# A kernel laid out by a planner: the planner's DMA model refitted, the early order searched again, two more blocks of x transposed by DMA

## The chip, the cores and the metric

The kernel runs on one core of a Trainium2 chip. The metric is the device time of one execution in microseconds (us), the median of several. Executions come with a state; only fast ones are compared, and where a profiled execution was of the slow state the text says so. TensorE is written PE, VectorE DVE, ScalarE ACT, GpSimd POOL, SyncE SP.

## The reference

Sliding-window attention with eight global keys, then a two-layer network with softplus on its output. Cut to what matters:

```python
# q, k, v: [4 batches, 8 heads, 768, 64];  w_in: [512, 2048];  w_out: [2048, 512]
scores = scale * q @ k^T + bias          # kept: 8 global keys, and the 96 keys up to the query
a      = softmax(scores)                 # bias: -slope[head] * distance
attn   = a @ v
x      = attn.transpose(0, 2, 1, 3).reshape(3072, 512)
h      = x @ w_in
out    = (relu(h) + log1p(exp(-abs(h)))) @ w_out        # softplus(h) @ w_out
```

## The kernel before

The 3072 tokens are 24 blocks of 128, or 12 windows of two blocks. For each window q, k and v are loaded (512 KB each), cast to bf16, transposed; each block gets scores, exp, the product with v (PV), a normalization and a transpose, which makes a piece of x. A window of x is then multiplied with w_in, goes through softplus and is multiplied with w_out. w_in and w_out come in four quarters of 512 KB each, cast on the way by GpSimd's DMA queue; everything else is loaded by SP's queue. Windows are counted from 0 in names.

No engine's order is written down by hand (the code below is shortened, cuts are marked by "..."). Some 900 operations, each with an engine, an estimated duration, what it needs and a rank, are put into an event simulation while the program is built. It issues at each engine the ready operation of lowest rank, and **the order that comes out is the order of the program**. In the traces DVE never overtakes: what stands first and waits holds up all behind it (in run e5 below DVE stands 4.32 us in front of one cast, and everything behind it comes later).

```python
SEEN = {"pe": 0.22, "dve": 0.1, "act": 0.1, "pool": 0.1, ...}     # us until another engine sees the end

def move(self, now):                      # model of the DMA engines: queues take turns, packet by packet
    heads = [q[0] for q in self.moving.values() if q]
    cycle = sum(h[2] for h in heads) / 1e3
    step = min(min(h[1] for h in heads), (now - self.moved) / cycle)
    ...
    op.end = self.moved + 0.7             # landed
    self.at(op.end + op.slack, lambda op=op: self.done(op))

def plan(self, busy):
    ...                                   # for each engine that is free at `now`:
    op = self.pick(e)                     # the ready operation of lowest rank
    if op is None and e == "pe" and now < self.filler_until: op = Op("filler", ...)   # multiplies zeros
    self.order.append(op)
    first = now + 1.3 if e == "sp" else op.end + 1.2      # first packet of a DMA
...
POOL_ORDER = "q1 in0 in1 out0 q2 out1 in2 in3 out2 out3".split()  # weights; "q1": wait for load q1
SP_ORDER = "in1 w2 in2 w3".split()        # "in1": wait for that quarter; "w2": load window 2
...
dur, dma = 0.55 * f + 0.05, (64 * f, 28)                          # a load of q, k or v
landed[s] = pl.add(f"w_{side}{s}", "pool", 0.78, ..., dma=(32, 98))   # a quarter: 32 packets, 98 ns each
...
f"castq{w}", {"dve": 0.69}, after=loaded[w, "q"]                  # cast of q of a window
f"oc{g}_{ns}", "dve", 0.69, after=[mm2s[g, last], ...], frees=[(mm2s[g, last - 3], "O")]
                                          # copy of an output block out of the one bank o_ps
for op in plan:
    op.fn(op)                             # emits the instructions in the planned order
```

`castq` waits for a load, and the copy `oc` frees the only bank that w_out products of the next output block can write.

The softmax here doesn't subtract the row's maximum and nothing guards it: scores larger than these inputs give would overflow.

## Time and profile before

| | before |
|---|---|
| median of 4 executions, and range | 219.44 us, 218.36 to 219.75 |
| span of the profiled execution | 217.1 us |
| first product with w_in | 18.46 us |
| PE's time lost in 0–24 / 24–60 / 60–84 / 84–98 / 98–120 / 120–132 / 132–end us | 11.08 / 1.59 / 0.31 / 0.38 / 0.30 / 0.11 / 0.90 |
| planned and real issue of the load of q7, us | 80.46, 81.51 |
| planned and real landing of q7, us | 84.59, 86.81 |

The loss is PE's spacing from one product to the next less the price of its kind, as the prediction prices them, with time for products of zeros counted as lost. I use 400 w_out records as the full count (11 windows of 32 and a last of 48), of which 31 lack a record in this trace (the prediction counted 384 and put 15 back, which comes to the same time, for of the last 48 some are narrower). Three of the 16 bias products lack a record too, all before 24 us; they are put back at 0.216 us each. The prediction counted 13, so its loss before 24 us is 0.65 us too large. "Planned" is the planner's own time for the operation; "real" is the trace's.

The prediction shows the page's rows and the start. Here is what it did not show, DVE's timeline around 87 us (start, length, line, operation):

```profile
86.83 0.69 DVE L564 COPY osb<-o_ps 128x512 f32<-128x512 f32 x1
87.55 1.23 DVE L424 TENSOR_TENSOR z<-s_ps,biasA 128x1024 f32<-128x1024 f32 x1
88.69 0.68 DVE L293 CAST qb<-q 128x1024 bf16<-128x1024 f32 x1
```

The copy of the output block comes first, then a bias addition, then the cast of q7. q7 landed at 86.81, 2.2 us later than planned, and nobody noticed. The table by stretch (us, PE, PEld, DVE, ACT, POOL, clock, DMA share, GB/s) has PE full there:

```profile
84.00:98.00 14.00, 13.84 (x150) 9.81 (x152) 11.13 (x21) 11.55 (x16) 5.53 (x9) 1.00 0.86 192
```

### The profile page before, as it was taken

How to read it: one execution, taken by the hardware profiler on the slowest of the kernel's cores; microseconds unless marked ns; L12 is line 12 of the kernel's file. 1: busy time of each engine (PE TensorE's matmuls, PEld its weight loads, DVE VectorE, ACT ScalarE, POOL GpSimd, SP SyncE). 2: the span in 40 equal slices, each digit the busy share in tenths (PEclk: the TensorE clock that was granted, in tenths of full speed). 3: DMA queues.
4: the chain of work that ended last, by engine and by line, in shares of the span. 5: the costliest groups of instructions: out<-in, count | busy, mean ns of one | idle time of the engine just before them, and what ended most of it. 6: DMA issues, size and time to landing. Idle time of an engine off the chain costs nothing.

```text
span 217.1 us, 5047 instructions
## 1 busy us (share of the span) xinstructions
PE 207.8 (96%) x2035; PEld 145.8 (67%) x2069; DVE 116.9 (54%) x251; ACT 156.0 (72%) x208; POOL 60.3 (28%) x117
## 2 busy tenths in 40 slices
PE   7599999999999999999999999999999999999994
PEld 6377875766677666667767767666766766776542
DVE  6575644728696685885544854654764763110120
ACT  4476885995969957888959669668768758857700
POOL 3570190014727170640404350332360000000000
PEclk9999999999999999999999999999999999999999
DMA  5999999999999986959577874987791211201102
GB/s 155 298 217 200 276 149 196 212 305 266 194 267 264 211 193 203 250 89 255 89 157 213 167 165 151 210 188 206 154 211 51 75 24 51 72 0 48 53 38 106
DMA packets 71511, 35.98 MB, mean 166 GB/s; under 512 B 27328, under 2 KB 68544, under 8 KB 71488
## 3 DMA queue, kind: packets, MB, share of 16 engines
q1 hardware_dynamic: 67120, 31.27, 62.1%
q0 software_dynamic: 4224, 4.19, 12.2%
q8 instruction: 16, 0.26, 0.5%
q10 hardware_dynamic: 144, 0.20, 0.2%
q14 instruction: 7, 0.06, 0.1%
HBM read 27.26 MB, written 6.29 MB: 155 GB/s over the span
## 4 chain that ended last, share of the span: by engine, by line
PE 82%; DMA 12%; SPq 2%; issue 1%; POOL 1%; ACT 0%; DVE 0%
PE h_ps L492 36%; PE o_ps L520 31%; DMA q<-in_q_dram 6%; PE s_ps L393 5%; PE x_ps L448 4%; DMA w_in_bf<-in_moe_w_in_dram 3%; PE s_ps L545 3%; DMA w_out_bf<-in_moe_w_out_dram 3%; PE s_ps L520 3%; SPq L286 1%; PE h_ps L470 0%; PE o_ps L545 0%; PE h_ps L319 0%; PE x_ps L445 0%; POOL w_in_bf L574 0%
## 5 line engine op out<-in xcount | busy, mean ns | idle before, releaser
L492 PE MATMUL h_ps<-XT,w_in_bf 128*128 128x256 bf16 x768 | 96.4, 273 | 0.3 <-ACT e L503 0.3
L492 PEld LDWEIGHTS <-w_in_bf 128*128 128x128 bf16 x768 | 73.2, 98 | 20.8 <-DMA w_in_bf<-in_moe_w_in_dram 0.5
L503 ACT ACTIVATE e<-h_ps 128x512 f32<-128x512 f32 x96 | 59.0, 629 | 29.5 <-PE h_ps L492 29.2
L520 PE MATMUL o_ps<-w_out_bf,g 128*128 128x512 bf16 x291 | 77.7, 379 | 1.4
L511 ACT ACTIVATE g<-e 128x1024 bf16<-128x1024 f32 x48 | 50.6, 1055 | 0.8
L520 PEld LDWEIGHTS <-g 128*128 128x128 bf16 x352 | 31.9, 98 | 23.8 <-issue 0.4
L430 ACT ACTIVATE pb<-z 128x1024 bf16<-128x1024 f32 (+1 forms) x40 | 39.1, 984 | 8.2 <-DVE z L424 7.9
L424 DVE TENSOR_TENSOR z<-s_ps,biasA 128x1024 f32<-128x1024 f32 x34 | 40.8, 1220 | 6.8 <-PE s_ps L393 6.2
L459 DVE RECIPROCAL rcp<-x_ps 128x4 f32<-128x4 f32 x44 | 7.9, 180 | 42.8 <-PE x_ps L448 38.8
L302 POOL CAST vb<-v 64x512 bf16<-64x512 f32 (+1 forms) x44 | 26.4, 600 | 14.0 <-DMA v<-in_v_dram 12.0
L302 POOL CAST kb<-k 64x512 bf16<-64x512 f32 x32 | 20.0, 627 | 34.9 <-DMA k<-in_k_dram 33.7
L564 DVE COPY osb<-o_ps 128x512 f32<-128x512 f32 x20 | 13.7, 686 | 25.7 <-PE o_ps L520 25.0
L460 DVE TENSOR_TENSOR xs<-x_ps,rcp 128x256 bf16<-128x256 f32 x44 | 18.7, 424 | 1.5
L448 PEld LDWEIGHTS <-pb 128*128 128x128 bf16 x320 | 14.5, 97 | 4.0
L393 PEld LDWEIGHTS <-kT 64*128 64x128 bf16 x352 | 10.0, 94 | 8.4 <-issue 7.2
L393 PE MATMUL s_ps<-qT,kT 64*128 64x128 bf16 x352 | 15.1, 218 | 0.0
L448 PE MATMUL x_ps<-vb,pb 128*128 128x65 bf16 x288 | 14.6, 193 | 0.0
L362 POOL COPY kT<-kT 128x32 bf16<-128x32 bf16 x16 | 3.3, 209 | 39.8 <-issue 20.2
L371 DVE COPY vb<-vb 4x512 bf16<-4x512 bf16 x32 | 10.3, 322 | 0.5
L434 ACT ACTIVATE pb<-s_ps 128x1024 bf16<-128x1024 f32 (+1 forms) x8 | 7.2, 916 | 4.6 <-PE s_ps L393 4.6
L293 DVE CAST qb<-q 128x1024 bf16<-128x1024 f32 x10 | 6.9, 690 | 5.3 <-DMA q<-in_q_dram 5.2
L646 PE MATMUL o_ps<-zeros 128*128 128x128 bf16 x85 | 8.0, 251 | 1.0 <-DVE zeros L599 1.0
(62 smaller groups left out, 97.6 us busy)
## 6 DMA issues: line engine op xcount, KB each, us to landing
out_dram<-osb SPq DMA_DIRECT2D x23, 256.0 KB, 2.6
q<-in_q_dram SPq DMA_DIRECT2D x11, 512.0 KB, 5.3
k<-in_k_dram SPq DMA_DIRECT2D x11, 512.0 KB, 5.7
v<-in_v_dram SPq DMA_DIRECT2D x11, 512.0 KB, 5.0
w_in_bf<-in_moe_w_in_dram POOLq DMA_DIRECT2D x4, 512.0 KB, 7.9
w_out_bf<-in_moe_w_out_dram POOLq DMA_DIRECT2D x4, 512.0 KB, 11.1
q<-in_q_dram SPq DMA_DIRECT2D x2, 256.0 KB, 4.3
k<-in_k_dram SPq DMA_DIRECT2D x2, 256.0 KB, 4.6
```

Source lines behind the costliest of these rows:

```text
L302: copy_on[eng](dst[64 * r : 64 * r + 64, hs, :], src)
L371: nc.vector.tensor_copy(vb_of(n - 1)[sl, :, 0:D], vb_of(first)[sl, :, 0:D])
L393: nc.tensor.matmul(s_t[:, 4 * sub + (lh // 2 if i == 0 else 2 * (lh // 2) + b), :], k_of(n - b, rows, m), q_of(n, rows, m), start=begin, s ...
L424: nc.vector.tensor_tensor(packed(n, z), rows_of(n, s_t), bias, ALU.add)
L430: nc.scalar.activation(pb[:, 0:nr, :], z[:, 0:nr, :], AF.Exp, scale=1.0 / root_d)
L448: nc.tensor.matmul(xv[:, lh, :], pb[:, 2 * j + b, :], vb_of(n - b)[:, h, :], start=b == 0, stop=b == 1,)
L460: nc.vector.tensor_tensor(xs[:, 4 * half : 4 * half + 4, :], xv[:, :, 0:D], rcp[:][:, :, None].to_broadcast([P, 4, D]), ALU.mult,)
L492: nc.tensor.matmul(hv[:, j, :], w_in_bf[:, m, fb * P : fb * P + P], XT[:, m, W * g : W * g + W], start=(m == 0), stop=(m == NM - 1),)
L503: nc.scalar.activation(e[:, p % 2, :].rearrange("p (a t r) -> p a r t", a=4, r=2), state["h", g, p][:].rearrange("p (a r t) -> p a r t", a ...
L511: nc.scalar.activation(gt[:, 4 * c : 4 * c + 4, :].rearrange("p a t -> p (a t)"), state["e", g, c][:].rearrange("p a t -> p (a t)"), AF.Ln ...
L520: nc.tensor.matmul(dst, state["g", g][:, fb, ns * P : ns * P + P], w_out_bf[:, fb, :], start=(fb == 0), stop=(fb == NFB - 1),)
L564: copy_on[eng](osb[:], src)
```

## The change

The intent: fit the planner's DMA model to traced transfers of the start, so that PE's order there meets the data where they really land; with the better model search a new early order of loads and weights; take eight more transposes from PE; halve four late loads. The arithmetic is the same. The diff, cut to its core:

```diff
+RANKS = {"Tq3.0": 9.51, "mm2_1_1.0": 10.15, ..., "mm1_0_0.0": -13.91, ...}    # 29 shifts of rank
+HALVED = "v10 q11 k11 v11".split()
+EARLY, MERGED, T_DMA, X_DMA = 4, 6, 4, 6
+SP_ORDER = "q0a k0a v0a k0b q0b q1 k1 v0b v1 in1 q2 k2 in2 k3 v2 q3 v3"
+POOL_ORDER = "q1 in0 in1 out0 in2 q2 in3 out1 out2 out3"
-    POOL_ORDER = "q1 in0 in1 out0 q2 out1 in2 in3 out2 out3".split()
-    SP_ORDER = "in1 w2 in2 w3".split()
+BASE = (-1.41, -18.64, 15.76, ...)            # other ranks of the first 14 blocks
+    LAP = {"dve": 0.08, "act": 0.1, "pool": -0.05, ...}    # an engine's next may start this early
+    FIRST = {"sp": 1.3, "pool": 1.9}                       # first packet after issue (pool: 1.2 before)
+    SLOW, SLOWER, SKEW = (3.6, 5.4), 1.8, 0.5              # slower packets early; landings + 0.5 to 51 us
-            f"w_{side}{s}", "pool", 0.78, lambda op: fn(s), rank, behind=[gate], dma=(32, 98)
+            f"w_{side}{s}", "pool", 0.78, lambda op: fn(s), rank, behind=[gate], dma=(32, 82)
-        if n < 8:                             # x transposed on PE
+        if n < X_DMA:                         # else by a transposing DMA
-                    after=[lns[0, p // 2], landed_out[...], mm2s.get((0, p - 1))],
+                    after=[lns[0, p // 2], landed_out[...]], behind=[mm2s.get((0, p - 1))],
...                                            # a few durations by 0.01 to 0.05 us
```

## The prediction

> **What bounds the kernel now.** I read the page first, then the table by stage, the timeline of TensorE over the first 60 us, the landings of the early transfers, and the list of waits. The page's busy and slice rows:
>
> ```profile
> PE 207.8 (96%) x2035; PEld 145.8 (67%) x2069; DVE 116.9 (54%) x251; ACT 156.0 (72%) x208; POOL 60.3 (28%) x117
> PE   7599999999999999999999999999999999999994
> DMA  5999999999999986959577874987791211201102
> ```
>
> TensorE (PE) is full from the third slice to the last (one slice is 5.4 us), and no other engine comes near. The DMA engines are full over the same early stretch, until slice 15, about 76 us. But a busy PE need not be doing useful work. The table by stage, first for all instructions (us, PE, PEld, DVE, ACT, POOL, clock, DMA share, GB/s), then for line 646 alone, which multiplies zeros to keep PE's clock up:
>
> ```profile
> 0.00:18.46 18.46, 14.43 (x199) 11.43 (x202) 12.17 (x49) 10.14 (x14) 8.83 (x26) 1.00 0.97 221
> 18.46:24.00 5.54, 5.49 (x85) 4.54 (x83) 3.13 (x12) 5.06 (x6) 0.42 (x2) 1.00 1.10 218
> 60.00:180.00 120.00, 118.90 (x1181) 83.16 (x1201) 75.87 (x144) 91.89 (x123) 36.98 (x67) 1.00 0.76 171
> ```
> ```profile
> 0.00:18.46 18.46, 7.76 (x83) 6.53 (x83) 1.00 0.97 221
> ```
>
> Of the 85 filler products 83 are before 18.46 us, where the first product with w_in starts. To get PE's useful work I priced each kind by its spacing in dense stretches of the timeline: 109 ns for a w_in product (256 columns), 216 ns for a w_out product (512), about 35 for a score, 30 for a PV product, 55 for a transpose, 216 or 109 for a bias product. Times the counts, with the 15 missing w_out records put back: 768 x 0.109 = 83.9; 384 x 0.216 = 82.9; 352 x 0.035 = 12.3; 352 x 0.030 = 10.6; 96 transposes 5.3; 13 bias products 2.3; 197 us together. PE's last product ends at 213.9, so 16.9 us are lost, and the closing copy and store take 3.2. Where the 16.9 lie, by summing the same prices window by window: 4.9 in 0 to 6 us, 4.2 in 6 to 12, 2.7 in 12 to 18, 0.9 in 18 to 24, about 2 in 24 to 60 (0.3 of it looks like a missing record), about 2.2 spread over the 150 us that follow. The start is therefore where there is something to win, and the rest is nearly bare work.
>
> Where 12 to 24 us goes, from PE's timeline (start, length, line, operation):
>
> ```profile
> 15.96 0.52 PE L470 MATMUL h_ps<-ident,xs 128*128 128x128 bf16 x4
> 16.32 1.22 PE L646 MATMUL o_ps<-zeros 128*128 128x128 bf16 x19
> 17.38 0.59 PE L378 MATMUL s_ps<-biasA,ident 128*128 128x512 bf16 x2
> 17.81 0.39 PE L646 MATMUL o_ps<-zeros 128*128 128x128 bf16 x4
> 18.13 0.40 PE L393 MATMUL s_ps<-qT,kT 64*128 64x128 bf16 x8
> 18.46 1.05 PE L492 MATMUL h_ps<-XT,w_in_bf 128*128 128x256 bf16 x8
> ```
>
> PE multiplies zeros 23 times (23 x 56 ns = 1.3 us) while w_in's first quarter, by its semaphore, landed at 17.13 and x of block 1 is out by 17.1 (copy at 16.69, 0.42 long). The first w_in product was simply put late in a fixed order. The second loss, in 30 to 48 us:
>
> ```profile
> 36.04 1.64 PEld L492 LDWEIGHTS <-w_in_bf 128*128 128x128 bf16 x16 [0.52 <-DMA w_in_bf<-in_moe_w_in_dram]
> 42.43 0.75 PEld L492 LDWEIGHTS <-w_in_bf 128*128 128x128 bf16 x7 [0.37 <-issue]
> ```
>
> w_in's third quarter (landed 36.00) is waited for half a microsecond, and once the exp that frees an h bank is late.
>
> **What the Trainium skill says.** Perfetto Trace Analysis, Identifying the Most-Contended Engine: matmul busy share is a poor measure of how near the roofline one is, and LDWEIGHTS busy share is a good one. The trace agrees in kind: 207.8 busy includes 8.0 us of fillers and overlapping tails, LDWEIGHTS is at 67%, so I count by spacing. TensorE: Matmul & The Clock Gate, Back-to-back issue gap: N/2.4 + 2.5 ns between isolated warm products, 109.2 for 256 columns and 215.8 for 512; the trace has just these spacings (8 in 0.87, 4 in 0.86), and not the lower ones that the same section gives for pipelined streams. DMA: Bandwidth & Descriptors, Issuing engines are not separate DMA queues: whatever engine issues, the transfers share the 16 engines and interleave. The trace agrees: q2, k2, v2 took 5.5 to 7.7 us to land from SP's queue beside the weights of GpSimd's queue, against 1.8 us of spacing between full loads while these had the engines alone (11.39, 13.18). So reordering transfers moves a landing only at the cost of another, except where the engines idle.
>
> **The change, part by part.** No arithmetic changes. The kernel's instruction streams are laid out by a planner while the program is built; the chip then follows that order and never reorders.
>
> (1) Order of early loads: k0's second half, q0's second half, q1, k1, then v0's second half, v1 (before: all of window 0 first). Landings before: 7.83, 8.71, v0's second half 9.60, q1 11.39, k1 13.18, v1 14.83. A half takes 0.88. So q1 should land at 10.5, k1 12.3, v0's second half about 13.2 or a little later, v1 15 to 16. The weights' gate is q1, so they are issued 0.9 earlier (10.7 instead of 11.57). But the bytes that must pass before w_in quarters 0 and 1 are complete are the same, and the engines have no gap there: quarter 0 stays at 16.5 to 17, quarter 1 at 19.3 to 19.7. Price: half 1 of blocks 0 and 1 waits for v: 13.2 + casts 0.7 + PV 0.3 + two normalizations 1.2 + transpose 0.4 + copy 0.6 = 16.4, still just before the weights.
>
> (2) Refitted planner: a weight packet 82 instead of 98, other latencies, new ranks for 29 operations, -13.91 among them for the first w_in product. It should now stand where its data land, 16.8 to 17.3 instead of 18.46. Gain: the 1.3 us of fillers seen above, less some for an order that misses: **1.2 us**.
>
> (3) w_in quarter 2 moves ahead of q2 into the first batch of weights, k3 follows it on SP before v2, q3, v3. Before, between 19.73 (quarter 1) and 29.40 (v2) 9.7 us passed for one w_out quarter (about 2.8) and three loads (5.4): some 1.4 us of DMA idle, which the longer queue fills. Quarter 2 lands at 26 to 28 instead of 36.0, window 3 some 5 us earlier; v2 comes later (34 to 37 instead of 29.4), but x of blocks 4 and 5 is first used by the products at 50.7, so that costs nothing. Gain: the 0.5 wait at 36.0 and a part of the other 1.2 us lost in 24 to 60: **0.6 us**.
>
> (4) x of blocks 7 and 8 (counted from one) by DMA: 8 PE transposes go, 8 x 55 ns = **0.44 us**, all of it on PE, which sets the end there. Two PSUM copies (0.42 on DVE, 0.58 on ACT) go too, beside other work. Two transposing DMAs come, 3.2 us to landing each in the median; x of these blocks is made around 60 to 64 us and used at 68.5, so hidden.
>
> (5) Four more halved loads (v10, q11, k11, v11): the same bytes in more DMAs, after 100 us, where the DMA share is 0.75 and less. PE waits for no load there: **0**.
>
> (6) `behind` instead of `after` between w_out products, scheduling overlaps, other estimates: planning only; order after 60 us changes a little. Only 2.2 us is lost there, so 0, plus or minus 0.4.
>
> Sum: 1.2 + 0.6 + 0.44 = 2.2, less 0.2 for small misses: 2.0 us off 219.27 gives **217.3 us**.
>
> **Rivals.** (A) The new wait takes the place of the old: v0's second half moves 3.6 us back and the margin computed in (1) is under a microsecond. If its casts, which share GpSimd with the weights' issue (0.8 us each), slip by 1.5 us, the first w_in product stands in front of a stalled PE and (2) is gone; the end would be 218.5 to 219. For it: GpSimd's four issues stand at about 10.7 to 14. Against: DVE can do the casts in 0.29 each. (B) The early order is already bound by bytes: DMA share is 1.1 to 1.2 from 6 to 48 us. Then w_in products start earlier but PE runs dry around 24 to 30, and only (4) and a little remain: 218.6. For it: the loads saturate. Against: from 18.46 on PE lost only 3 us in the next 40 with the old order. (C) It goes better: the search also removes half of the 4.2 us lost in 6 to 12, where PE idles 2.6 us for a cast of q by GpSimd (8.44, 0.61 long, though q landed at 7.83). 0.5 to 1.5 more, 216. (D) A plan fitted too closely: ACT at 93% in 42 to 48 us, so earlier w_in products meet late exps, and PE waits for h banks; up to +1, 218.3 or, with (A), over 219.
>
> **Range and chances.** My sum with none of the rivals is 217.3; A or B gives up to 219, C 215.8. Eight in ten: 215.7 to 218.9. Over 2% is 4.39 us, below 214.9: it would need a third of all that PE loses before 24 us, most of which is waiting for first data at 3.76 us that the change does not move. Chance 0.06. Slower by 2% (over 223.7) would need a real stall after 60 us: 0.03. Within 2%: 0.91.
>
> **What would show it.** Right: first w_in product at 16.5 to 17.5; fillers down from 85 to about 60; no PE wait for w_in at 36; 24 transposes of x instead of 32; the rest from 60 us to the end shorter only by what was gained before. Wrong: PE waiting for v or for w_in between 14 and 20 us (A), PE's loss in 24 to 48 above 1.5 us (B or D), or idle time on PE after 60 us that was not there (a late DMA transpose of x, step 4).

## The result, and the profile after

The changed kernel took **222.01 us** in the median of 4 executions (220.71 to 222.79), before 219.44 in the same rounds. Ratios are the mean time of one kernel's fast runs over that of the other's fast runs of the same rounds, so not quite the ratio of the medians: 1.0115, 95% interval 1.0071 to 1.0159. Two further runs of it gave 1.0100 and 1.0106. So the change costs about 1.1%, 2.3 us over the three runs; 217.3 had been predicted.

| us | before | after |
|---|---|---|
| first product with w_in | 18.46 | 17.86 |
| products of zeros | 85 | 77 |
| PE's loss 0–24 | 11.08 | 10.03 |
| 24–60 | 1.59 | 3.26 |
| 60–84 | 0.31 | 0.41 |
| 84–98 | 0.38 | **2.20** |
| 98–120 | 0.30 | 0.22 |
| 120–132 | 0.11 | **1.18** |
| 132–end | 0.90 | 0.69 |
| PE's last product ends, real | 213.89 | 216.76 |
| the same, planned | 214.05 | 212.86 |

The losses rise by 3.3 us in all; less the 0.44 us of transposes that went, this is the 2.9 us by which PE's last product comes later. The last two lines say most. Before, the chip was 0.2 us ahead of the plan at the end. The new plan is 1.2 us shorter, and the chip comes 3.9 us after it. From the page, the rows that answer to those of the prediction:

```profile
PE 210.3 (96%) x2053; PEld 145.5 (66%) x2053; DVE 119.0 (54%) x256; ACT 158.4 (72%) x209; POOL 55.4 (25%) x109
PE   7989997999999999799999999999999999999994
DMA  5999999999849997749969785975954211300112
```

PE is still at 96%. The slices (5.5 us each) give the places away: two sevens that were nines, the seventh slice, 33 to 38 us, and the seventeenth, 88 to 93. The waits of PE (line waited at, who released it: us in total, times, longest) name the places:

```profile
PE o_ps L552 <- DVE osb L596: 1.5, 2, 1.3
PE h_ps L502 <- DVE xs L492: 1.1, 2, 0.7
PE h_ps L524 <- DMA w_in_bf<-in_moe_w_in_dram: 1.1, 1, 1.1
```

None of the three stood in the list of before, where only the weight loads had waited 0.5 us for w_in. The middle one belongs to the early part: 0.7 us at 15.7 and 0.4 us at 26.0, each in front of a normalization.

**The start looks better, but that is chance.** The timeline of PE:

```profile
17.18 0.42 PE L480 MATMUL x_ps<-vb,pb 128*128 128x65 bf16 x8
17.53 0.40 PE L425 MATMUL s_ps<-qT,kT 64*128 64x128 bf16 x8
17.86 1.92 PE L524 MATMUL h_ps<-XT,w_in_bf 128*128 128x256 bf16 x16
```

Sixteen w_in products follow at once, with no products of zeros between. By these two traces 1.05 us are won at 24 us. But three later runs (e5, e15, e17) have the start of before unchanged, and their traces contradict it. First a wait of PE in before, then the same wait and the first w_in product in e5:

```profile
9.11 0.40 PE L319 MATMUL h_ps<-ident,qb 128*128 128x128 bf16 x4 [2.61 <-POOL qb L293]
```
```profile
8.13 0.40 PE L319 MATMUL h_ps<-ident,qb 128*128 128x128 bf16 x4 [1.35 <-POOL qb L293]
17.49 1.05 PE L492 MATMUL h_ps<-XT,w_in_bf 128*128 128x256 bf16 x8
```

In the trace of before the first half of v0 landed at 6.93 us, in e5 at 6.07. GpSimd casts it first and then the q that PE waits for, so all of PE came 1 us later in the one trace of before that the prediction read. The first w_in product of the old start stands at 18.46, 17.49, 17.62 and 19.70 us in four traces (the last with 3.4 us of half clock from 9.96 on), that of the new start at 17.80 to 18.50 in six (after, a0, e18, e16, e1, e6). PE's loss in 0–24 is 11.1, 10.1, 10.2 and 12.2 against 10.0 to 10.7. No gain of the new start is shown.

**About 1 us or more is lost at 36 us.** The loss in 24–60 is 1.5 to 2.2 us in the four traces with the old start and 2.5 to 3.6 in the six with the new one.

```profile
35.05 0.40 PE L425 MATMUL s_ps<-qT,kT 64*128 64x128 bf16 x8
36.56 1.05 PE L524 MATMUL h_ps<-XT,w_in_bf 128*128 128x256 bf16 x8 [1.12 <-DMA w_in_bf<-in_moe_w_in_dram]
```

PE waits 1.12 us for the last quarter of w_in (in3). The landings tell why (us; from the trace of each):

| | before: issued, landed | after: issued, landed | after, planned landing |
|---|---|---|---|
| w_in quarter 0 | 11.57, 17.13 | 10.07, 17.10 | 17.38 |
| w_in quarter 1 | 12.45, 19.73 | 10.95, 19.68 | 20.00 |
| w_in quarter 2 | 27.48, 36.00 | 12.71, 25.16 | 25.98 |
| **w_in quarter 3** | 28.21, 38.49 | 27.08, **36.52** | **34.79** |
| w_out quarter 1 | 26.75, 32.55 | 27.97, 40.05 | 38.31 |
| w_out quarter 3 | 29.77, 45.37 | 29.43, 47.40 | 45.35 |

The first batch lands up to 0.9 us before its plan. Everything in the second batch of weights lands 1.7 to 2.1 us after its plan. in3 was issued at 27.08, but the first packet on GpSimd's queue moved at 30.73, 3.7 us later, while k2, k3, v2 and q3 were on SP's queue, issued and not landed; in the two batches of before this took 1.7 and 1.4 us. Over all 20 traces it goes with the number of loads that SP had issued and that had not landed: 1.4 to 2.0 us with two of them, 2.1 to 3.0 with three, 3.0 to 3.7 with four (13 batches each; no run varied this alone). The new order issues more of them. After that the two queues alternate packet for packet: in the trace each gets about 140 packets per us, which are 140 KB/us for the weights' 1 KB packets and 70 KB/us for the loads' 512 B ones. The Trainium skill says the same of turns (DMA: Bandwidth & Descriptors, Queues, rings and completion order: round-robin between queue rows, at packet granularity); that the first turn may take 3.7 us it doesn't say there.

**The rest is lost behind a cast.** DVE and PE around 89 us:

```profile
88.36 0.69 DVE L325 CAST qb<-q 128x1024 bf16<-128x1024 f32 x1 [2.01 <-DMA q<-in_q_dram]
88.97 0.18 DVE L491 RECIPROCAL rcp<-x_ps 128x4 f32<-128x4 f32 x1
89.18 0.42 DVE L492 TENSOR_TENSOR xs<-x_ps,rcp 128x256 bf16<-128x256 f32 x1
89.52 0.68 DVE L596 COPY osb<-o_ps 128x512 f32<-128x512 f32 x1
```
```profile
90.25 1.02 PE L552 MATMUL o_ps<-w_out_bf,g 128*128 128x512 bf16 x4 [1.33 <-DVE osb L596]
```

For q7 the order is now the other way round from before: first the cast of q7, then a normalization, then the copy out of o_ps. DVE stands 2.01 us in front of q7, and PE stands 1.33 us in front of the copy, whose data had been ready. q7 landed at 88.24; the plan had it at 83.73, so putting the cast first looked free. The same again with q9, planned 118.91, landed 123.44:

```profile
123.56 0.70 DVE L325 CAST qb<-q 128x1024 bf16<-128x1024 f32 x1 [2.70 <-DMA q<-in_q_dram]
124.17 2.35 DVE L456 TENSOR_TENSOR z<-s_ps,biasA 128x1024 f32<-128x1024 f32 x2
126.44 0.68 DVE L596 COPY osb<-o_ps 128x512 f32<-128x512 f32 x1
```

For q9 the cast stood ahead of the copy in before too. There q9 landed at 120.03, 0.3 us after its plan, and nothing waited:

```profile
121.67 0.68 DVE L293 CAST qb<-q 128x1024 bf16<-128x1024 f32 x1
122.51 0.69 DVE L564 COPY osb<-o_ps 128x512 f32<-128x512 f32 x1 [0.16 <-PE o_ps L520]
```

So it takes both: a cast ahead of the copy, and data that come late against the rest.

How q7 came to be 4.5 us late is read by setting the real issue of each DMA on SP's queue beside its planned issue:

| us after the plan | after | before |
|---|---|---|
| issue of q4's first transpose | 1.4 | −0.3 |
| issue of k5 | 2.4 | 0.5 |
| issue of v6 | 3.1 | 1.0 |
| issue of q7 | 3.6 | 1.1 |
| landing of q7 | 4.5 | 2.2 |
| landing of q9 | 4.5 | 0.3 |

After starts the 50s with the delay of the weights (1.4), and SP's queue, which is as much in a fixed order as the others, adds to it in steps. The last 0.9 us is in the flight of q7. In both traces a 16 KB packet of the instruction queue is on one DMA engine near 82 us (0.9 us before, 1.3 after), and the transfers dip then. There are 16 such packets in each trace, one every 9 to 19 us; that this one made q7 late is a guess.

### The profile page after: what moved, and what is told of

It reads as the page before. It is cut to its first block, busy times and chain, and to the rows that moved or that the text cites.

```text
span 219.7 us, 5068 instructions
## 1 busy us (share of the span) xinstructions
PE 210.3 (96%) x2053; PEld 145.5 (66%) x2053; DVE 119.0 (54%) x256; ACT 158.4 (72%) x209; POOL 55.4 (25%) x109
## 4 chain that ended last, share of the span: by engine, by line
PE 60%; DMA 21%; DVE 6%; SPq 5%; POOL 3%; issue 2%; ACT 0%; DVEq 0%; POOLq 0%
PE h_ps L524 26%; PE o_ps L552 24%; DMA q<-in_q_dram 8%; DMA w_out_bf<-in_moe_w_out_dram 7%; DMA k<-in_k_dram 4%; SPq L318 3%; DMA v<-in_v_dram 3%; PE x_ps L480 3%; PE s_ps L577 3%; PE s_ps L425 3%; PE s_ps L552 2%; DVE z L456 2%; DVE osb L596 1%; POOL kb L334 1%; POOL vb L334 1%
## 5 line engine op out<-in xcount | busy, mean ns | idle before, releaser
L552 PE MATMUL o_ps<-w_out_bf,g 128*128 128x512 bf16 x320 | 79.8, 379 | 1.5 <-DVE osb L596 1.5
L462 ACT ACTIVATE pb<-z 128x1024 bf16<-128x1024 f32 (+1 forms) x40 | 39.6, 991 | 7.3 <-DVE z L456 7.0
L334 POOL CAST vb<-v 64x512 bf16<-64x512 f32 (+1 forms) x37 | 22.8, 616 | 40.0 <-DMA v<-in_v_dram 38.4
L480 PE MATMUL x_ps<-vb,pb 128*128 128x65 bf16 x304 | 15.8, 193 | 0.9 <-ACT pb L462 0.4
L403 DVE COPY vb<-vb 4x512 bf16<-4x512 bf16 x32 | 11.3, 355 | 3.2 <-PE x_ps L480 2.7
L325 DVE CAST qb<-q 128x1024 bf16<-128x1024 f32 (+1 forms) x10 | 6.7, 666 | 5.9 <-DMA q<-in_q_dram 5.9
```

The source lines that it names most:

```text
L334: copy_on[eng](dst[64 * r : 64 * r + 64, hs, :], src)
L403: nc.vector.tensor_copy(vb_of(n - 1)[sl, :, 0:D], vb_of(first)[sl, :, 0:D])
L462: nc.scalar.activation(pb[:, 0:nr, :], z[:, 0:nr, :], AF.Exp, scale=1.0 / root_d)
L480: nc.tensor.matmul(xv[:, lh, :], pb[:, 2 * j + b, :], vb_of(n - b)[:, h, :], start=b == 0, stop=b == 1,)
L552: nc.tensor.matmul(dst, state["g", g][:, fb, ns * P : ns * P + P], w_out_bf[:, fb, :], start=(fb == 0), stop=(fb == NFB - 1),)
```

## The experiments

The theories, by the letters of the expectations. **A**: the fixed order puts a cast of q ahead of an output copy, q lands later than planned, and PE pays; this is the late loss. **C**: the two new transposing DMAs of x push the loads back and so cause it. **E**: the wait for in3 is not worth its 1.1 us, for it is passed on. **F**: the refit of the planner, not the new order or the DMAs of x, is what made the plan too tight. **H** and **I** concern PE's clock and are explained at the end. Losses are PE's, in us, from the one profiled execution of each.

### Move the two casts, in either kernel

```diff
+    plan = later(plan, ['castq7.0', 'Dq7.0'], 'oc3_0.0')          # e1: after, cast behind the copy
+    plan = later(plan, ['castq9.0', 'Dq9.0', 'Dq9.1'], 'oc5_0.0')
     for op in plan:
         op.fn(op)
```

> The changed kernel with two casts on VectorE moved, nothing else: the cast of q of window 7 behind the first output copy of group 3, that of window 9 behind the first output copy of group 5. No load, no order on any other engine changes. Theory A (VectorE works in a fixed order; its cast stands in front of the copy that frees TensorE's output bank and waits for a q that lands 4.5 us after the plan): the stalls of 1.9 us at 88 to 93 and 0.9 us at 125 to 129 go, so 2.3 to 2.8 us faster than the changed kernel, about 219.4, the same as before. Theory B (the late data themselves hold TensorE, through the scores of window 7): under 0.5 us gained, the wait only moves to the scores. VectorE's waits show which.

Measured 219.76 us, ratio 1.0060 (1.0034 to 1.0087). The loss in 84–98 fell from 2.20 to 0.27, in 120–132 from 1.18 to 0.20. But a loss of 1.28 appeared in 98–120, where there had been 0.22: PE waited 0.7 for a normalization. So by the times the two casts are worth about 1.0 us (1.0107, the mean of the three runs of the changed kernel, to 1.0060), less than the 2.3 to 2.8 expected: the place was right, and a part of the lateness was passed on.

```diff
+    plan = earlier(plan, ["castq7"], "norm101")                   # e5: before, cast ahead of the copy
```

> The kernel before, with the cast of q of window 7 moved ahead on VectorE, in front of the normalization and of the output copy of group 3 that it follows there. All else as before. Theory A: the stall appears where there was none: q lands at about 86.8, the normalization waited for at 84.4 and the copy at 86.8 come 2 to 3 us later, so 1 to 3 us slower than before. Theory B: no change, as q lands where it did.

Measured 221.9 us, ratio 1.0154 (1.0139 to 1.0168): one instruction of 0.69 us moved on an engine that is 54% busy, and the kernel is 3.4 us slower. Its waits, and its DVE:

```profile
PE o_ps L520 <- DVE osb L564: 2.0, 1, 2.0
```
```profile
85.48 0.69 DVE L293 CAST qb<-q 128x1024 bf16<-128x1024 f32 x1 [4.32 <-DMA q<-in_q_dram]
86.09 0.18 DVE L459 RECIPROCAL rcp<-x_ps 128x4 f32<-128x4 f32 x1
...
88.71 0.69 DVE L564 COPY osb<-o_ps 128x512 f32<-128x512 f32 x1
```

DVE stands 4.32 us in front of q7 and PE 2.0 in front of the copy. That this order makes this stall is shown from both sides. How much of the 2.3 us it explains is less sure: e1 won 1.0, and e7, below, wins all of it by a plan made anew.

### Are the new DMAs of x to blame?

```diff
-EARLY, MERGED, T_DMA, X_DMA = 4, 6, 4, 6
+EARLY, MERGED, T_DMA, X_DMA = 4, 6, 4, 8
```

> The changed kernel with x of blocks 7 and 8 transposed on TensorE again, everything planned anew from there (the plan is the same until about 53 us, and plans an end 0.46 later). Theory C (the two transposing DMAs hold up SyncE's queue, 1.3 us each, ahead of k5, v5, q6, and that is why q of window 7 is late): k5 lands 2 to 3 us earlier than the 68.2 of the changed kernel, q7 before 86, and the 88 us stall goes; 1 to 2 us faster than the changed kernel. Rival (the lateness comes from the wait for w_in and from slow transfers): q7 still late, at most 0.5 us faster; the new plan can also put the cast elsewhere, which the order of cast and copy shows.

Measured 222.87 us, ratio 1.0169 (1.0133 to 1.0206): slower, not faster. The profiled execution was slow, so I take only positions from it: q7 landed at 87.76, hardly earlier than the 88.24 of after, although k5 came 3.1 us earlier. And the plan, made anew, put the cast 4.6 us ahead of the copy. Theory C fell. The run taught something about method too: any change of an input to the planner lays out everything behind it anew, so "one part undone" is never one part only.

### Put another operation in front of in3

```diff
+    plan = later(plan, ['mm1_0_7.0'], 'scores50.0')    # this product behind a w_out product and scores
```

> The changed kernel with one w_in product of TensorE (the first that needs the fourth quarter of w_in, which waits 1.1 us at 36.5) moved behind the w_out product and the scores that follow it. Theory D (the loss at 35 us is one of order): TensorE works through the wait, 1.2 us of lag gone at 45 us, though later waits can eat it. Theory E (bytes: the next quarters of w_out land at 40.05, 43.65 and 47.4, whatever TensorE does): the wait is only passed on to the next product with w_out's second quarter, lag at 45 us stays within 0.3 of the changed kernel's 1.7, time within 0.5 us of it.

Measured 221.5 us, ratio 1.0119 (1.0079 to 1.0159): no gain. The wait for w_in is gone, and PE waits 1.0 us, in two waits, for w_out instead. This fits Theory E: what is missing at 36 us is weights, whoever asks for them.

### The same kernel once more

> The changed kernel itself once more, so that the runs beside it have it on the same chip. Every theory: 1.0 to 1.5% slower than before, stalls at 35, 88 to 93 and 125 us again (they come from the fixed order).

Measured 221.46 us, ratio 1.0100 (1.0059 to 1.0141). The eight executions go from 219.59 to 223.63, the six fast ones to 222.3; the profiled one was slow. In the same rounds 44 fast executions of before go from 217.73 to 220.36. The standard deviation of the fast ones is 1.2 us against 0.7, from six executions.

### Tell the planner that late loads are late

```diff
             after=after, behind=[chain], takes=takes, dma=dma,
+            slack=3.5 if w > 4 else 0.0,
```

The planner now believes that every load of windows 5 to 11 lands 3.5 us after what its model says. Its planned end stays where it was (213.25 for the whole program): the margin costs the plan nothing.

> The changed kernel, its planner told that loads of windows 5 and later land 3.5 us later than it works out, planned anew. The planned end does not move (213.25 in both), the casts of q of windows 7 and 9 now stand behind the output copies. Theory A (orders planned without margin for late loads): all stalls of TensorE between 60 and 210 us go, 2 to 2.8 us off the changed kernel and steadier from run to run, so 0 to 0.4% slower than before (what is left is the wait at 35 us). Theory B (late data themselves): under 0.7 us off.

Measured 218.73 us, ratio **0.9999** (0.9980 to 1.0018), and on another chip later:

> The version with margin once more, beside the previous one on the same chip: ratio to before 0.997 to 1.003 (it was 0.9999).

218.47 us, ratio 0.9973 (0.9955 to 0.9991). One line, and the plan that follows from it, takes back all that the change had lost. In the profile the cast stands 2.5 us behind the copy, and neither waits; q7 landed at 88.25, as late as ever:

```profile
87.71 0.69 DVE L596 COPY osb<-o_ps 128x512 f32<-128x512 f32 x1
...
90.18 1.01 DVE L325 CAST qb<-q 128x1024 bf16<-128x1024 f32 x1
```

The losses are 0.27, 0.23 and 0.18 in 84–98, 98–120 and 120–132. The wait for in3 is still there (0.9), and PE's last product ends at 213.57, 3.2 us before that of after.

### The same, with the loads behind the weights

```diff
-SP_ORDER = "q0a k0a v0a k0b q0b q1 k1 v0b v1 in1 q2 k2 in2 k3 v2 q3 v3"
+SP_ORDER = "q0a k0a v0a k0b q0b q1 k1 v0b v1 in1 q2 k2 in2 v2 in3 q3 k3 v3"     # on top of the margin
```

> As the previous one, and SyncE holds q, k, v of window 3 until the last quarter of w_in has landed, v of window 2 going first. Theory E (the wait at 35 us is one of bytes and of who gets the engines first; three loads pass before the weights): the last quarter of w_in lands at 33 to 34.5 instead of 36.5, those of w_out some 2 us earlier too, the wait of 1.1 us at 36 goes, and 1 to 1.7 us more is won than by the previous run: faster than before by 0.3 to 0.8%. If the weights land no earlier, Theory E is wrong on who holds them up, and the time is that of the previous run.

Measured 219.5 us, ratio 1.0031 (1.0009 to 1.0053). In3 landed at 35.91, 0.4 to 0.7 us earlier than in e7b and e7, not the 2 to 3.5 expected; w_out's last three quarters came 1.0 to 2.5 us earlier. PE no longer waits for w_in, but q3 lands at 45.85 instead of 41.49, and the loss in 24–60 is the same (2.77 against 2.86). So nothing was won on PE. That the start is bound by the bytes that must pass, whoever goes first, is argued from two orders only, not shown.

### The refit alone

The new model, with everything else as before: old orders, old ranks, x on PE, no halved loads.

```diff
-RANKS = {"Tq3.0": 9.51, ...}
-HALVED = "v10 q11 k11 v11".split()
-EARLY, MERGED, T_DMA, X_DMA = 4, 6, 4, 6
+RANKS = {}
+HALVED = []
+EARLY, MERGED, T_DMA, X_DMA = 4, 6, 4, 8
+SP_ORDER = "q0a k0a v0a q0b k0b v0b q1 k1 v1 in1 q2 k2 v2 in2 q3 k3 v3"     # the order of before
+POOL_ORDER = "q1 in0 in1 out0 q2 out1 in2 in3 out2 out3"                     # the order of before
+BASE = (-39.74, -33.92, ...)                                                 # that of before
```

> The refitted planner alone: early order, ranks and window ranks as before, x of blocks 7 and 8 on TensorE, all loads whole. Its plan puts the cast of q of window 7 4 us ahead of the output copy that it followed before. Theory F (the refit, not the early order or the x transfers, makes the late orders fragile): a stall at 85 to 92 us as in the changed kernel, TensorE's idle time there over 1.5 us, and 0.5 to 1.5% slower than before. Rival (the early order is what pushes the loads late): no stall at 88 us, time within 0.4% of before.

Measured 222.06 us, ratio **1.0161** (1.0133 to 1.0188). This is the largest single fact: the model that was meant to be better, under the old orders and ranks, costs 3.5 us (0.0161 of the 218.9 us that before took there). Its waits:

```profile
PE o_ps L545 <- DVE osb L589: 1.3, 1, 1.3
PE o_ps L344 <- DVE kb L318: 1.1, 1, 1.1
```

The same kind of stall, at other places: at 75 us an output copy again, behind a cast of q that DVE stood 1.88 us in front of (the loss in 60–84 is 1.80), and a cast of k at 28 us. At 84–98, where Theory F had put its stall, only 0.7 us is lost. So F holds in its core, that the refit alone costs as much, and missed the place; about half of the added loss lies before 60 us. All that the change added to the refit, taken together, won about 1.2 us (1.0161 to 1.0107). As x by DMA alone is worth about that much (e10), the new early order and ranks won nothing here that stands out of the noise.

### What the parts are worth when the plan has its margin

All three are on top of the margin of e7.

```diff
-EARLY, MERGED, T_DMA, X_DMA = 4, 6, 4, 6
+EARLY, MERGED, T_DMA, X_DMA = 4, 6, 4, 8                                     # e10
```

> The version with the 3.5 us margin on later loads (same time as before, 0.9999), with x of blocks 7 and 8 transposed on TensorE again. Part 4 alone, with no stall to hide it. If x by DMA is worth the 8 transposes (0.44 us) and costs nothing, as predicted: 0.2 to 0.5 us slower than the version with margin, ratio to before 1.001 to 1.0025. If the transposing DMAs cost more on SyncE's queue than they save: faster than it, ratio under 0.999. The planner itself says 0.95 slower.

219.6 us, ratio 1.0039 (1.0019 to 1.0059). x by DMA gains 0.9 us against e7 (0.9999), and 1.2 against the mean of e7 and e7b (0.9986). The planner had said 0.95; the prediction's 0.44 is the transposes alone.

```diff
+RANKS = {}                                                                   # e11
+SP_ORDER, POOL_ORDER, BASE = ...                                             # those of before, as in e9
```

> The version with margin, with the early order, the ranks and the window ranks of before. Part 1 to 3 undone, x by DMA and the refit kept. If the early order's gain (1.1 us of work ahead at 30 us) is given back at 35 us by the wait for weights that land later, as the traces of the changed kernel show: within 0.7 us of the version with margin, ratio 0.997 to 1.003. If the early order is worth what the planner says (2.6 us between these two plans): ratio 1.009 to 1.013.

220.23 us, ratio 1.0080 (1.0056 to 1.0103). The early orders with their ranks gain about 1.8 us against e7 on this planner with its margin; without the margin (e9 against the changed kernel) hardly anything was left for them. Even with the margin this kernel is slower than before: the ranks of before had been found with the old model and don't suit the new one.

```diff
-HALVED = "v10 q11 k11 v11".split()
+HALVED = []                                                                  # e12
```

> The version with margin, with no additional halved load (v10, q11, k11, v11 whole). The orders of TensorE and ScalarE are the same. All theories: no change, ratio within 0.002 of the version with margin (0.9999).

219.17 us, ratio 1.0010 (0.9990 to 1.0030): the halved loads do nothing that these runs can tell.

### Two attempts to go below the kernel before

```diff
+SP_ORDER = "q0a k0a v0a k0b q0b k1 q1 v0b v1 k2 q2 in2 in1 v2 q3 v3 k3"          # e13, with the margin,
+POOL_ORDER = "q1 in0 in1 out0 in2 q2 out3 out1 in3 out2"                         # and weights modelled later
```

> The version with margin, and the planner taught what the traces show of the weights (second batch: first packet some 3 us after the issue when SyncE's queue is long, landing 0.9 later), the early order searched again under it: k2 and q2 directly behind v1, the last quarters of w_out and w_in in another order. If the wait at 35 us is what keeps the version with margin from beating before: 1 us faster than before, ratio 0.994 to 0.998. If the new order trades it for a later start of the w_in products (planned at 19.9 instead of 17.6): no better than before, ratio 1.000 to 1.006.

221.27 us, ratio 1.0107 (1.0068 to 1.0147). The searched order was a miss: the first w_in product came at 21.45 us, and 12.07 us are lost by 24 (four bias products without a record put back).

```diff
+    slack=1.7 if (side, s) == ("in", 3) or side == "out" and s > 0 else 0.0      # e14: second batch of weights;
+RANKS, BASE = searched again with this
```

> The version with margin, its planner also told that the second batch of weights lands 1.7 us later than it works out (as traced), and the ranks searched again under these two corrections (plan 213.68 for TensorE's end; the old ranks give 214.59 under the same corrections). If the version with margin fails to beat before only because its order expects the weights too early at 35 us: 0.5 to 1.2 us faster than the version with margin, ratio to before 0.994 to 0.998. If the second batch's bytes are the limit whatever the order: no better than the version with margin, 0.998 to 1.003.

218.86 us, ratio 0.9983 (0.9956 to 1.0010). Telling the planner the truth about the second batch too takes the loss in 24–60 down to 2.24 and, in this one trace, gives it back at the start (11.67 in 0–24, first w_in product at 19.50). No version is clearly faster than before; the best, the change with the margin, is equal to it within 0.3%.

### How large is a stall?

The profiled e5 lost 4.2 us in 84–98 although PE waited 2.0. The records of the granted clock show it at 0.50 from 90.89 to 94.30, 3.4 us, just after that wait. The Trainium skill knows this (TensorE: Matmul & The Clock Gate, What's actually happening, and Why this matters for your kernels): the clock halves after an idle window, and gaps of PE above some 3 us are to be avoided. Theory H: the half clock adds 1.7 us to the stall, and makes the spread of the changed kernel. Rival I: only the wait counts. e15 puts products of zeros into the wait, and e17 is e5 again on the same chip.

```diff
+    spares = [Op("spare", "pe", 0.058, lambda op: nc.tensor.matmul(x_ps[:, 384:512], zeros[:], zeros[:]), 0.0)
+              for _ in range(36)]
+    at = next(j for j, o in enumerate(plan) if o.name == "mm2_3_4")      # the w_out product that waits
+    plan = plan[:at] + spares + plan[at:]
```

> The same kernel without the zeros, on the same chip. H and I: 1.0154 again (219.0 to 222), half clock for 3.4 us after a wait of PE of about 2 us.

> The kernel before with the cast of q of window 7 ahead of its output copy (as in the earlier run of that edit, which lost 3.3 us), and with 36 products of zeros (2.0 us) on PE just ahead of the w_out product that waits. Theory H: of the 4.2 us that PE lost between 84 and 98 us in that run, 2.0 were the wait and 1.7 the half clock that the records show from 90.85 to 94.25, after it (3.4 us at 0.50). With zeros in the wait the clock stays at 1.00, the loss falls to about 2.5 us and the time from 1.0154 to about 1.0076 of before. Rival I: the wait alone costs, and the record of the clock is a mark of it: time unchanged at 1.0154, or longer by what the zeros add.

e17: 223.76 us, ratio 1.0198 (1.0147 to 1.0250). e15: 222.06 us, ratio 1.0152 (1.0114 to 1.0189). The stretches of e17, then of e15 (columns as above; the clock is the third from the end):

```profile
91.00:92.00 1.00, 0.17 (x1) 0.10 (x1) 0.94 (x3) 0.97 (x3) 0.94 (x2) 0.94 0.27 62
92.00:93.00 1.00, 1.00 (x3) 0.30 (x2) 1.00 (x1) 1.00 (x2) 0.23 (x1) 0.50 0.64 190
93.00:94.00 1.00, 1.00 (x10) 0.34 (x8) 0.04 (x1) 1.00 (x2) 0.00 (x0) 0.50 1.16 372
```
```profile
91.00:92.00 1.00, 0.99 (x14) 0.41 (x13) 0.85 (x2) 1.00 (x3) 0.00 (x0) 1.00 0.96 287
92.00:93.00 1.00, 1.00 (x13) 0.53 (x12) 0.97 (x4) 1.00 (x2) 0.00 (x0) 1.00 1.14 372
```

With zeros in the wait the clock stays, and the loss in 84–98 is 3.0 us against 4.6 (e17) and 4.2 (e5). In the profile H is right: the clock stays, and the loss falls by 1.2 to 1.6 us, of 1.7 expected. In the times the two kernels are 0.5% apart with intervals that overlap, and e15 alone isn't below e5's 1.0154, so the 1.7 us are shown in the traces and not in the times; and e5's four executions, two of them at a mean clock of 0.99 and two at 1.00, all took 221.75 to 221.97. Four of e15's six executions have a mean clock of 0.992, which is what one spell of 3.4 us at half would give (1 − 0.5 × 3.4 / 219), somewhere that the profile of a fifth execution doesn't show.

> The changed kernel itself on the same chip, for the comparison with the run with zeros. H and I: 1.010 to 1.012, runs from 219.5 to 223.7.

> The changed kernel with 36 products of zeros on PE just ahead of the w_out product that waited 1.33 us in its first profile and 2.12 us in its second (the second with half clock for 3.4 us after it). H: runs whose wait passes some length between 1.3 and 2.0 us lose another 1.7 us, which makes the wide spread of this kernel (219.6 to 223.6 us in twelve runs); with zeros no half clock, mean ratio 1.006 to 1.009 instead of 1.0108, highest run under 222.5. I: mean and spread as without the zeros (ratio 1.010 or more, runs to 223.5).

The changed kernel without zeros: 220.87 us, 1.0106 (1.0068 to 1.0144). With them: 221.03 us, 1.0100 (1.0063 to 1.0137). No difference. And all six executions of the one without zeros had a clock of 1.00 and yet went from 220.48 to 222.61. So H fell where it mattered: the half clock isn't what costs the changed kernel its 1.1%, nor what spreads it. Its profiled waits at this place, 1.33 and 1.39 us in the two fast ones, left the clock at 1.00.

## Why the prediction was wrong

By its own steps:

(1) **Early order of loads: right.** q1, k1, v0's second half and v1 landed at 9.89, 11.70, 12.58 and 14.82; the prediction had 10.5, 12.3, 13.2 and 15 to 16. Quarters 0 and 1 landed at 17.10 and 19.68 as predicted, at the same time as before. Rival A came in small: PE stood 0.72 us at 15.7 in front of a normalization of the half that needs v0's second half, and the last x that the first w_in product needs was copied out by 17.46, where the step had 16.4.

(2) **Refitted start, 1.2 gained: not shown, and its ground was chance.** The first w_in product came at 17.86 us (16.8 to 17.3 predicted) and there were 77 products of zeros (about 60 predicted). The step read the zeros in front of the first w_in product as "simply put late in a fixed order". In e5 the same order has this product at 17.49, 0.42 us after quarter 0 landed at 17.07: there was little to win. The trace that the step read was 1 us late because of one landing. e11 puts early order and ranks together at 1.8, which is the sum of (2) and (3), but e9 against the changed kernel leaves next to nothing for them, so the agreement is luck.

(3) **Quarter 2 early, 0.6 gained: wrong in sign in the place.** Quarter 2 did land early (25.16). But the wait moved to the next quarter, in3, which PE reached at 35.4 and which landed at 36.52; the loss in 24–60 rose from 1.59 to 3.26. The step counted the DMA engines' idle 1.4 us as a gain for the quarter that moved ahead and left out the one that moved behind it. The prediction named above 1.5 us in 24 to 48 as the mark of rival B or D (it is 3.0), and it looks like B: no weights landed between 25.16 and 36.52.

(4) **x of blocks 7 and 8 by DMA, 0.44: right in sign, too small.** The runs give 0.9 to 1.2; where the rest comes from is open.

(5) **Halved loads, 0: right.**

(6) **"Planning only; order after 60 us changes a little … so 0, plus or minus 0.4": this is the step that failed.** The refit, taken alone and without the new ranks, cost 3.5 us (e9, which holds the new packet times of step 2 and the estimates and `behind` of step 6 together; no run parts them), and in the changed kernel the two stalls behind casts, 84–98 and 120–132, lost 2.9 us more than before. The argument had been that only 2.2 us were lost after 60 us, so there was little to gain, which is true; it doesn't follow that there was little to lose. The profile of before had the evidence: q7 landed 2.2 us later than its plan and nothing waited, because the cast stood behind the copy. The order was tolerant of lateness, and the step took that for a fact of the kernel and not of the order. It was luck of the order, not design: for q9 before had the cast in front as well. The chances had 0.03 for "a real stall after 60 us"; there were two, and they cost less than the 4.4 us that 2% needs.

Rival D, "a plan fitted too closely", was right in its heading. It looked for ACT and h banks, up to 1 us, in the first 48 us. The stalls were DVE's, behind loads, after 84.

What stays open: why before's old ranks suit the new model so badly that e11 is slower than before even with the margin; why e1's removed stalls left 1.28 us in 98–120; whether any order passes the second batch of weights faster; which part of the refit makes the late order; and what spreads the times of the changed kernel at a full clock. That the instruction packet near 82 us makes q7 late is a guess from the traces; before has the packet too, and no run took it away.

## What to carry to other kernels

In a program of fixed orders, ask of each operation that waits for a DMA what stands behind it on its engine: one 0.69 us cast moved ahead of a copy, on an engine that is half idle, cost 3.4 us (1.7 us of it may be the half clock that followed). A model that orders a program should err late on arrivals: a late guess may cost nothing (3.5 us of margin left the planned end unchanged), an early one stalls all that is behind, so fit the transfers of the stretch that you optimize and keep the margins elsewhere. Before trusting a plan, set planned beside real issue and landing through the whole run; a lag that grows, 1.4, 2.4, 3.1, 3.6 us here, is the warning, and the loss by stretch says where it is paid. And before building on one trace, look at a second execution: what the prediction wanted to win at the start, 1.2 us, was mostly one late landing.

## What the Trainium skill lacked or had wrong

- DMA: Bandwidth & Descriptors says that all issuers share the 16 engines and that queue rows take turns by packets, and the traces agree (about 140 packets per us for each of two queues, so 140 and 70 KB/us for 1 KB and 512 B packets). It gives about 1 us to the first byte on GpSimd's path and lacks what loads in front do to it: the first packet of a newly issued batch moved 1.4 to 2.0 us after its issue with two of SP's loads issued and not landed, 2.1 to 3.0 with three, 3.0 to 3.7 with four (39 batches in 20 traces).
- TensorE: Matmul & The Clock Gate puts the fall to half clock at an idle window of about 3.4 us and warns of gaps above some 3 us. Here waits of PE of 2.0, 2.1, 2.5 and 3.7 us were each followed by 3.4 us at 0.50, waits of 1.3 to 1.4 us were not. At the start a wait of 2.6 us (before) was not, and one of 1.6 us was in e17 and was not in e15. So length alone doesn't decide, and 2.0 us can be enough.
- The pages know the transfers of instructions, but none has them as a cause of late loads. Here each of 16 packets of 16 KB takes 0.9 to 1.5 us on one engine; one of them, near 82 us, lies beside a load that lands late in both kernels. That it is the cause is not shown.
- Perfetto Trace Analysis offers LDWEIGHTS' busy share (and the share of peak FLOPs) in place of matmul busy, and nothing here speaks against it: it fell from 67.2% to 66.2% while matmul busy stayed at 96% and the time rose by 1.1%. Where the time went the spacing summed by stretch showed.
